# Top-k attention with an MLP behind it: row limits for four blocks at once, and row blocks taken by twos

## The chip, the cores and the metric

The kernel runs on one core of a Trainium2 chip. Its time is what the device takes for one execution, in microseconds (us); of several executions the median stands. One execution was also recorded by the hardware profiler. The core's engines work at the same time and meet through semaphores: PE multiplies matrices (its weight loads are listed as PEld), ACT applies functions with a scale and a bias, DVE works on vectors, POOL does the same more slowly, and SP issues DMA transfers. Each has its own list of instructions and works it off in order.

## The reference

`q`, `k` and `v` have 8 batches of 8 heads with 576 rows of 64. For each head, scores are `q k^T / 8`. In each row only the scores that reach the row's 32nd largest are kept. A softmax over them weighs `v`. The heads of a token are joined to 512 features, and an MLP follows with a parametric ReLU:

```python
kth = np.partition(scores, -32, axis=-1)[..., -32:-31]
scores = np.where(scores >= kth, scores, -1e9)
attn = softmax(scores);  x = join_heads(attn @ v)          # 4608 x 512
h = x @ w_in                                               # 4608 x 2048
out = (np.maximum(h, 0) + alpha * np.minimum(h, 0)) @ w_out
```

## The kernel before

Two heads form a pair; there are 32 pairs. The 576 rows of a pair's two heads make nine row blocks of 128: blocks 0 to 7 are four blocks of each head in turn, and block 8 holds the last 64 rows of both. All pairs together have 288 row blocks. `ORDER` lists them: pair after pair up to block 251, and mixed across the four pairs of the last batch from block 252 (`N0`) on.

The program writes out the order of every engine's instructions by hand. It counts ticks `n`, one a row block, and each stage of a block has its tick:

- PE computes scores in f32 into a PSUM tile (`scores`, L328), one tick ahead. Block `n` and its follower form a unit of two; a block 8 whose follower is not a block 8 too is a unit of one.
- ACT writes `b = scores + NT0` (`act_b`, L337). `NT0` is an estimate of the row's limit, from mean and variance of its scores, with its sign turned. ACT then sums the signs of `b` (`act_s`, L343): how many scores of the row lie above the estimate. It takes the exponential of a whole unit in one operation (`act_e`, L348).
- One tick on, POOL turns the sum into a flag `SG` (L353), and DVE turns the sign of `b` where the flag says that the wanted limit lies below the estimate (`flip`, L359).
- Two ticks on (`LAG_S`), DVE finds the eight largest of each of six segments of 96 columns (L369). Three ticks on (`LAG_M`), it merges these 48 into the 24 largest, in order (`merge_ops`, L384 and L386). The two are interleaved.
- Every three blocks DVE picks the limits. ACT has made the rank `ra` from the sum of signs (`sel_a`, L392). DVE compares it with a table of 24 numbers (`sel_eq`, L397), multiplies by the sorted list (`sel_pr`, L403), sums (`sel_sum`, L407) and turns the sign back (`limit`, L413).
- Seven ticks on (`LAG_W`), DVE makes the mask `b >= limit` (`mask`, L433), and POOL multiplies it with the exponentials (L443, `weights`). The last six blocks have both done by DVE in one operation (L440). SP issues the DMA that transposes the weights (L456, L452 for block 8).
- Behind that, by ticks after the mask: PE multiplies with `v` (`av`, L494), DVE takes the reciprocal of the sums (L511), ACT scales the result into `xb` (L523), SP transposes `xb`, and `feed` puts the MLP of the finished rows on a queue.

PE takes from that queue at each tick: steps cost credits (0.9 for a hidden step, L697; 1.5 for each third of an output block, L711 and L715), and a tick gives 1.9 credits, 2.4 from tick 288. Up to tick 253 at most one step a tick is taken. What is left two ticks after the last weights are due is flushed (`flush`), and the last 128 rows go through a path of their own (`last_ph`, L583; `last_pz`, L603).

Ahead of each pair, `prep_plan` spreads its preparation over the ticks before its first block (`BASE`): transposes of `q` and `k` on PE with copies on ACT, a product matrix (`pg`), its product with `q` (`pr0`, `pr1`), DVE's elementwise product `P` (L246), sums by PE into `st`, and seven small operations of ACT and DVE (L266 to L288) that end in `NT0` (`dve_6`). Pairs 11 to 19 are prepared a pair's length earlier, pairs from 20 on two lengths (`LEAD1`, `LEAD2`). `act_v` copies `v` to bf16 (L203) from a staging tile that `load_v` fills.

PSUM is shared out in pools: `ps_s` (scores, two tiles), `ps_d` (two banks: `pr0`, `pr1`, `st` and the products `pu` of `av`), `ps_a` (one bank: `pq`, `pk`, `pt`, `pg`) and `ps_m` (one, the MLP).

At the end `checks` tests the row limits and the estimates over all blocks; a flag decides on a general path (`general_batch`), none of which appears in the trace.

Of the kernel before, what the change touches and what calls it, by code (L numbers as in the profile page):

```python
# [16 lines left out]
S = 576  # L17
NSEG = 6
SEG = S // NSEG
KW = 24  # L20
TINY = 1.0e-30
ZSQ = 0.640625
M2MAX = 96.0
# [9 lines left out]
def kernel(  # L33
# [36 lines left out]
    ident_b = const.tile([128, 128], BF16, name="ident_b")  # L70
    nc.gpsimd.tensor_copy(ident_b, ident_f)
# [6 lines left out]
    iota = const.tile([128, KW], FP32, name="iota")  # L78
# [28 lines left out]
    M2 = prep.tile([128, NT], FP32, name="M2", bufs=1)  # L107
# [3 lines left out]
    st_vs = [prep.tile([128, 10, D], FP32, name=f"st_v{i}", bufs=1) for i in range(2)]  # L111
# [5 lines left out]
    def early_sets():  # L117
# [4 lines left out]
        for t_ in st_vs:  # L122
            nc.vector.memset(t_[64:128, 4, :], 0.0)
            nc.vector.memset(t_[0:64, 5, :], 0.0)
# [4 lines left out]
        for i in range(KW):  # L129
            nc.vector.memset(iota[:, i:i + 1], (1.0 + 2 * i) ** 2)  # L130
# [3 lines left out]
    def load(p, eng2=None):  # L134
# [10 lines left out]
        pairs[p] = dict(q=st_q, k=st_k, st_v=st_vs[p % 2], v=v_bfs[p % NV])  # L145

    def load_v(p):
        hA = 2 * p
        st_v = st_vs[p % 2]
# [25 lines left out]
    def prep_plan(p):  # L175
# [26 lines left out]
        def act_v():  # L202
            nc.scalar.copy(d["v"][:, :, 0:D], d["st_v"])  # L203
# [66 lines left out]
        def dve_2():  # L270
            nc.vector.tensor_tensor(d["sq"], M2[:, ns], d["sq"], ALU.subtract)

# [18 lines left out]
        if p == 1:  # L291
            ts = [-9, -8, -7, -6, -5, -4, -3, -2, -2, -2, -2, -2, -1, -1, 1]
        else:
            ts = [-14, -13, -12, -11, -10, -9, -7, -6, -5, -5, -4, -4, -3, -2, -8]
# [5 lines left out]
                 dict(dve=[dve_6]), dict(act=[act_v])]  # L300
# [29 lines left out]
    def act_b(n0):  # L330
        m = unit_of[n0][1]
        b = attn.tile([128, m, S], FP32, name=f"b{m}", bufs=5 if m == 2 else 1)
# [6 lines left out]
        tiles[n0]["bu"] = b  # L339
# [5 lines left out]
    def act_e(n0):  # L345
        m = unit_of[n0][1]
        e = attn.tile([128, m, S], BF16, name=f"e{m}", bufs=4 if m == 2 else 1)
        nc.scalar.activation(e, tiles[n0]["bu"], AF.Exp, scale=scl)  # L348
        for i in range(m):
            tiles[n0 + i]["e"] = e[:, i, :]  # L350
# [21 lines left out]

    Ls, sel, KPs = {}, {}, {}

    def merge_ops(n):
        C = Cs[n // TPP][:, n % TPP, :, :].rearrange("p g e -> p (g e)")
        if n % 3 == 0:
            Ls[n // 3] = attn.tile([128, 3, KW], FP32, name="L", bufs=2)
        L = Ls[n // 3][:, n % 3, :]
# [10 lines left out]
    def sel_a(m):  # L390
        a = attn.tile([128, 3], FP32, name="ra", bufs=2)
        nc.scalar.activation(a, S_all[:, 3 * m:3 * m + 3], AF.Square, bias=c513)  # L392
        sel[m] = a

    def sel_eq(m):
        EQ = attn.tile([128, 3, KW], FP32, name="EQ", bufs=1)
        nc.vector.tensor_tensor(EQ, sel[m].unsqueeze(2).to_broadcast([128, 3, KW]),  # L397
                                iota.unsqueeze(1).to_broadcast([128, 3, KW]), ALU.is_equal)
        sel[m] = EQ

    def sel_pr(m):
        L = Ls.pop(m)
        nc.vector.tensor_tensor(L, sel[m], L, ALU.mult)  # L403
        sel[m] = L

    def sel_sum(m):
        nc.vector.tensor_reduce(out=KK[:, 3 * m:3 * m + 3], in_=sel.pop(m), op=ALU.add,  # L407
                                axis=mybir.AxisListType.X)

    def limit(m):  # L410
        ms = slice(3 * m, 3 * m + 3)
        KPs[m] = attn.tile([128, 3], FP32, name="KP", bufs=4)
        nc.vector.scalar_tensor_tensor(out=KPs[m].bitcast(I32), in0=KK[:, ms].bitcast(I32),  # L413
                                       scalar=FLIP, in1=SG[:, ms], op0=ALU.bitwise_xor,
                                       op1=ALU.bitwise_xor)

    def row_limit(n):
        return KPs[n // 3][:, n % 3:n % 3 + 1]
# [39 lines left out]
    xb, xm = {}, {}  # L458
# [101 lines left out]

    t7 = 7 * S
    CL = t7 % NX + 64 + 384

    def turn_last(h):
        pool, tag = (ps_a, "pa") if h == 0 else (ps_m, "misc")
        xa = pool.tile([128, 2, 128], BF16, name="xa", tag=tag)
        for j in range(2):
            c0 = 128 * (2 * h + j)
            nc.tensor.transpose(xa[:, j, :], xb[B - 1][3][:, c0:c0 + 128], ident_b)
        nc.vector.tensor_copy(xT[:, 2 * h:2 * h + 2, CL:CL + 128], xa)  # L570

    lastc = {}
# [173 lines left out]
    LAG_S, LAG_M, LAG_W = 2, 3, 7  # L746
# [3 lines left out]
    with tc.manual_schedule(engines={E.PE, E.Activation, E.DVE, E.Pool, E.SP}):  # L750
# [73 lines left out]
        load_v(1)  # L824
# [8 lines left out]
        for wn in range(NT):  # L833
            wdue.setdefault(wn + LAG_W if wn < NW else 3 * (wn // 3) + 7, []).append(wn)
        n = 0
        end = max(NT + 24, 0)
        while n < end or back or after:
            for p in range(2, NPAIR):
# [25 lines left out]
            if n >= 3 and n % 3 == 0 and n - 3 < NT:  # L864
                sel_a((n - 3) // 3)
# [18 lines left out]
            for wn in due:  # L884
                if wn < NW:
# [4 lines left out]
            for wn in due:  # L890
                weights(wn, wn >= NW)
# [6 lines left out]
            pick = bool(merges) and mn % 3 == 2  # L898
            if pick and n >= NT:
                sel_eq(mn // 3)  # L900
            lm = n - LAG_M - 3
# [6 lines left out]
            if 0 <= lm < NT and lm % 3 == 0:  # L908
                limit(lm // 3)
            if pick and n < NT:  # L910
                sel_eq(mn // 3)
# [3 lines left out]
            if pick:  # L915
                sel_pr(mn // 3)
                held = [lambda m=mn // 3: sel_sum(m)]
                if mn % TPP == TPP - 1:
                    put(n + 2, "dve" if mn < NT - 1 else "end", lambda g=mn // TPP: check_group(g))
                    if mn == NT - 1:  # L920
                        put(n + 2, "end", checks)
# [143 lines left out]
```

## Time and profile before

| | |
|---|---|
| median of 3 runs | 872.82 us (871.4 to 875.64) |
| the profiled execution's own time | 873.98 us |
| its span, first to last instruction | 872.1 us |
| DVE busy | 835.1 us (96%) |
| ACT busy | 790.3 us (91%) |
| PE busy | 721.9 us (83%) |
| POOL busy | 431.0 us (49%) |
| granted PE clock, mean | 0.943 |

Busy time counts overlapping instructions of an engine once. A group's row has the line, engine and operation, what is written and read with the shape, the count, then the busy time in us, the mean duration of one in ns, and the idle time in front with what ended it. A row in order of time has the start and duration in us. An engine that is full in a stretch limits it; one that is not may still hold it up by coming late.

### The profile page before, as it was taken

The numbers are of one execution on the slowest core, as the hardware profiler recorded it, in microseconds if no ns is written. First come the engines' busy times: TensorE is split into PE (matmuls) and PEld (weight loads), VectorE is DVE, ScalarE is ACT, GpSimd is POOL, SyncE is SP. The second block draws the span as 40 slices with busy tenths as digits, with TensorE's granted clock in tenths as the row PEclk, the third lists the DMA queues.
The fourth block names the chain that finished last, engine by engine and source line by source line (L and its number), as shares of the span: only waits on it lengthen the run. The fifth ranks groups of instructions, "written<-read, shape, count | busy, mean of one in ns | idle before, by whom it ended". The sixth has DMA issues, their size and how long they took to land.

```text
span 872.1 us, 20608 instructions
## 1 busy us (share of the span) xinstructions
PE 721.9 (83%) x5697; PEld 428.3 (49%) x5771; DVE 835.1 (96%) x5188; ACT 790.3 (91%) x1873; POOL 431.0 (49%) x630
## 2 busy tenths in 40 slices
PE   6776688778978789787987789977897988899996
PEld 4443444334554345444454445643455554566674
DVE  4999999999999999999999999999999999999992
ACT  6999999999999999889999999989999899979861
POOL 1455545555454555545555455554554555544530
PEclk9997779899979999989998999989999999999999
DMA  7999644644665545564576445475455543535442
GB/s 161 156 178 199 131 89 90 126 91 97 135 139 107 108 102 116 100 135 95 114 154 115 98 97 116 111 136 98 92 128 121 121 103 81 106 71 100 91 96 56
DMA packets 342619, 99.37 MB, mean 114 GB/s; under 512 B 334672, under 2 KB 334944, under 8 KB 342496
## 3 DMA queue, kind: packets, MB, share of 16 engines
q1 hardware_dynamic: 340144, 95.58, 54.4%
q0 software_dynamic: 1152, 2.10, 2.0%
q8 instruction: 47, 0.77, 0.4%
q14 instruction: 76, 0.62, 0.2%
q10 hardware_dynamic: 1200, 0.30, 0.2%
HBM read 36.71 MB, written 9.44 MB: 53 GB/s over the span
## 4 chain that ended last, share of the span: by engine, by line
DVE 62%; ACT 21%; PE 12%; DMA 2%; issue 1%; POOL 1%; SPq 0%; DVEq 0%; another core or an unknown queue 0%; ACTq 0%
DVE C L369 20%; DVE y L359 9%; DVE mk L433 9%; DVE C L386 8%; DVE L L384 7%; ACT b L337 5%; ACT h L343 5%; ACT e L348 4%; PE ps L328 4%; PE pz L715 3%; PE ph L697 2%; ACT gT L703 2%; DVE P L246 2%; ACT xb L523 2%; PE pu L494 1%
## 5 line engine op out<-in xcount | busy, mean ns | idle before, releaser
L443 POOL TENSOR_TENSOR w<-mk,e 128x576 bf16<-128x576 bf16 x250 | 319.3, 1277 | 337.9 <-DVE mk L433 187.5
L369 DVE MAX8 C<-y 128x8 f32<-128x96 f32 x1728 | 419.1, 243 | 0.1
L328 PE MATMUL ps<-qkT 64*128 64x288 f32 (+1 forms) x1280 | 256.5, 474 | 35.1 <-ACT b L337 34.6
L337 ACT ACTIVATE b<-ps,NT 128x576 f32<-128x576 f32 x288 | 202.3, 761 | 3.1 <-PE ps L328 3.1
L343 ACT ACTIVATE h<-b 128x576 bf16<-128x576 f32 x288 | 202.9, 705 | 1.7
L697 PE MATMUL ph<-xT,w_in_b 128*128 128x128 bf16 (+2 forms) x997 | 150.4, 292 | 40.8 <-ACT gT L703 33.6
L328 PEld LDWEIGHTS ps<-qkT 64*128 64x128 f32 (+1 forms) x1280 | 134.3, 194 | 97.6 <-ACT b L337 59.8
L348 ACT ACTIVATE e<-b 128x1152 bf16<-128x1152 f32 (+1 forms) x158 | 174.2, 1102 | 0.0
L384 DVE MAX8 L<-C 128x8 f32<-128x48 f32 x864 | 162.6, 188 | 0.1
L359 DVE TENSOR_SCALAR y<-b,SG 128x576 int32<-128x576 int32 x288 | 147.0, 510 | 8.2 <-POOL SG L353 7.8
L433 DVE TENSOR_SCALAR mk<-b,KP 128x576 bf16<-128x576 f32 x282 | 143.6, 509 | 0.0
L715 PE MATMUL pz<-w_out_b,gT 128*128 128x512 bf16 x543 | 132.4, 380 | 1.2 <-issue 0.5
L697 PEld LDWEIGHTS <-w_in_b 128*128 128x128 bf16 x1024 | 80.4, 100 | 104.0 <-issue 79.6
L703 ACT ACTIVATE gT<-ph 128x512 bf16<-128x512 f32 x140 | 86.0, 621 | 28.1 <-PE ph L697 28.1
L386 DVE MATCH_REPLACE8 C<-L,C 128x48 f32<-128x48 f32 x576 | 108.3, 188 | 0.0
L715 PEld LDWEIGHTS <-gT 128*128 128x128 bf16 x560 | 51.6, 98 | 68.5 <-issue 14.0
L494 PE MATMUL pu<-v_bf,wT 128*128 128x65 bf16 (+1 forms) x1600 | 69.4, 198 | 14.4 <-DMA wT<-w 6.9
L494 PEld LDWEIGHTS <-wT 128*128 128x128 bf16 (+1 forms) x1600 | 65.2, 103 | 25.6 <-issue 10.2
L353 POOL TENSOR_SCALAR SG<-S_all 128x1 int32<-128x1 f32 x288 | 65.3, 227 | 18.9 <-ACT h L343 18.8
L443 POOL TENSOR_TENSOR wm<-mk,e 128x576 bf16<-128x576 bf16 x32 | 40.8, 1276 | 49.9 <-DVE mk L433 45.6
L343 ACT ACTIVATION_READ_ACCUMULATOR h<-b 128x1 f32 x288 | 62.8, 218 | 0.0
L523 ACT ACTIVATE xb<-pu,rz 128x64 bf16<-128x64 f32 x224 | 54.5, 369 | 0.0
(113 smaller groups left out, 728.1 us busy)
## 6 DMA issues: line engine op xcount, KB each, us to landing
out_dram<-o_sb SPq DMA_DIRECT2D x34, 256.0 KB, 2.3
st_q<-in_q_dram SPq DMA_DIRECT2D x64, 128.0 KB, 2.8
st_v<-in_v_dram SPq DMA_DIRECT2D x64, 128.0 KB, 2.6
kst<-in_k_dram SPq DMA_DIRECT2D x62, 128.0 KB, 2.6
w_stage<-in_moe_w_out_dram SPq DMA_DIRECT2D x16, 256.0 KB, 3.1
w_in_b<-in_moe_w_in_dram POOLq DMA_DIRECT2D x8, 256.0 KB, 6.4
wT<-w SPq DMA_TRANSPOSE x128, 3.3
st_q<-in_q_dram SPq DMA_DIRECT2D x32, 32.0 KB, 2.5
```

The lines of the kernel that those rows point to most:

```text
L328: nc.tensor.matmul(o_, l_, r_, start=True, stop=True)
L337: nc.scalar.activation(t["b"].rearrange("p (a c) -> p a c", a=2), t["ps"], AF.Identity, bias=NT0[:, p * TPP + j:p * TPP + j + 1], scale=ON ...
L343: nc.scalar.activation(h, tiles[n]["b"], AF.Sign, accum_out=S_all[:, n:n + 1])
L348: nc.scalar.activation(e, tiles[n0]["bu"], AF.Exp, scale=scl)
L359: nc.vector.tensor_scalar(t["y"].bitcast(I32), t["b"].bitcast(I32), FLIP, SG[:, n:n + 1], ALU.bitwise_xor, ALU.bitwise_xor)
L369: return [lambda g=g: nc.vector.max(out=C[:, n % TPP, g, :], in_=t["y"][:, g * SEG:(g + 1) * SEG]) for g in range(NSEG)]
L384: ops.append(lambda r=r, src=src: nc.vector.max(out=L[:, 8 * r:8 * r + 8], in_=src))
L386: ops.append(lambda r=r, src=src: nc.vector.match_replace(out=C2, in_to_replace=L[:, 8 * r:8 * r + 8], in_values=src, imm_value=NEG))
L433: nc.vector.tensor_scalar(t["mk"], t["b"], row_limit(n), None, ALU.is_ge)
L443: nc.gpsimd.tensor_tensor(dst, t["mk"], t["e"], ALU.mult)
L697: nc.tensor.matmul(hold[f][:, i, :], w_in_b[:, kk, (f + i) * 128:(f + i + 1) * 128], xT[:, kk, c0:c0 + tb], start=(kk == 0), stop=(kk == N ...
L715: nc.tensor.matmul(pz[0:m], hold["gT"][:, f, r0:r0 + m], w_out_b[:, f, :], start=False, stop=(f == NFT - 1))
```

## The change

- Limits are picked for groups of four row blocks up to block 251 and of three from 252 on (`GROUPS`). Masks and weights stand `z + 4` ticks behind their block: eight in groups of four, seven in groups of three. Where two masks fall due in one tick (blocks 251 and 252), the second is fused on DVE.
- The rank is the absolute value of the shifted sum in place of its square, and table, rank and comparison result are bf16.
- Units of two run on across the border of a pair; only block 8 and the last block are units of one. There are six tiles `b` and five tiles `e`, all of two blocks, where there were five and four, and one of each of a single block.
- `pr0` moves from the two banks of `ps_d` to the one of `ps_a`, for pairs from 2 on.
- `M2` is bf16 and only checked; the subtraction `dve_2` reads `st` in PSUM instead.
- `dve_6` runs a tick earlier, behind the flip of that tick. `act_v` runs three ticks later (five ticks earlier for pair 1), and `load_v` two ticks later for most pairs, both through one staging tile in place of two.
- The bf16 identity matrix is made at tick 288 in a tile that the sign pass leaves.

```diff
-M2MAX = 96.0
+M2MAX = 95.5
...
-    ident_b = const.tile([128, 128], BF16, name="ident_b")
-    nc.gpsimd.tensor_copy(ident_b, ident_f)
...
-    iota = const.tile([128, KW], FP32, name="iota")
+    iota = const.tile([128, KW], BF16, name="iota")
...
-    M2 = prep.tile([128, NT], FP32, name="M2", bufs=1)
+    M2 = prep.tile([128, NT], BF16, name="M2", bufs=1)
...
-    st_vs = [prep.tile([128, 10, D], FP32, name=f"st_v{i}", bufs=1) for i in range(2)]
+    st_v = prep.tile([128, 10, D], FP32, name="st_v", bufs=1)
...
         for i in range(KW):
-            nc.vector.memset(iota[:, i:i + 1], (1.0 + 2 * i) ** 2)
+            nc.vector.memset(iota[:, i:i + 1], 1.0 + 2 * i)
...
-        m = 1 if ORDER[n][1] == 8 and ORDER[n + 1][1] != 8 else 2
+        m = 1 if n in (8, NT - 1) else 2
...
-            if nm == "pr0":
+            if nm == "pr0" and p < 2:
                 pool, tag = ps_d, "pd"
...
-            nc.vector.tensor_tensor(d["sq"], M2[:, ns], d["sq"], ALU.subtract)
+            nc.vector.tensor_tensor(d["sq"], d["st"][:, 0, :], d["sq"], ALU.subtract)
...
         if p == 1:
-            ts = [-9, -8, -7, -6, -5, -4, -3, -2, -2, -2, -2, -2, -1, -1, 1]
+            ts = [-9, -8, -7, -6, -5, -4, -3, -2, -2, -2, -2, -2, -1, -1, -4]
         else:
-            ts = [-14, -13, -12, -11, -10, -9, -7, -6, -5, -5, -4, -4, -3, -2, -8]
+            ts = [-14, -13, -12, -11, -10, -9, -7, -6, -5, -5, -4, -4, -3, -3, -5]
...
-                 dict(dve=[dve_6]), dict(act=[act_v])]
+                 {dvx: [dve_6]}, dict(act=[act_v])]
...
-        b = attn.tile([128, m, S], FP32, name=f"b{m}", bufs=5 if m == 2 else 1)
+        b = attn.tile([128, 2, S], FP32, name="b", bufs=6)
...
-        e = attn.tile([128, m, S], BF16, name=f"e{m}", bufs=4 if m == 2 else 1)
-        nc.scalar.activation(e, tiles[n0]["bu"], AF.Exp, scale=scl)
+        e = attn.tile([128, 2, S], BF16, name="e", bufs=5)
+        nc.scalar.activation(e[:, 0:m, :], tiles[n0]["bu"], AF.Exp, scale=scl)
...
+    GZ = 4
+    GROUPS = [(i, GZ) for i in range(0, N0, GZ)] + [(i, 3) for i in range(N0, NT, 3)]
+    group_of = {i: (g, z) for g, z in GROUPS for i in range(g, g + z)}
...
-    def sel_a(m):
-        a = attn.tile([128, 3], FP32, name="ra", bufs=2)
-        nc.scalar.activation(a, S_all[:, 3 * m:3 * m + 3], AF.Square, bias=c513)
-        sel[m] = a
-
-    def sel_eq(m):
-        EQ = attn.tile([128, 3, KW], FP32, name="EQ", bufs=1)
-        nc.vector.tensor_tensor(EQ, sel[m].unsqueeze(2).to_broadcast([128, 3, KW]),
-                                iota.unsqueeze(1).to_broadcast([128, 3, KW]), ALU.is_equal)
-        sel[m] = EQ
+    def sel_a(g, z):
+        a = attn.tile([128, GZ], BF16, name="ra", bufs=2)
+        nc.scalar.activation(a[:, 0:z], S_all[:, g:g + z], AF.Abs, bias=c513)
+        sel[g] = a[:, 0:z]
+
+    def sel_eq(g, z):
+        EQ = attn.tile([128, GZ, KW], BF16, name="EQ", bufs=1)[:, 0:z, :]
+        nc.vector.tensor_tensor(EQ, sel[g].unsqueeze(2).to_broadcast([128, z, KW]),
+                                iota.unsqueeze(1).to_broadcast([128, z, KW]), ALU.is_equal)
+        sel[g] = EQ
...
+    def make_ident_b():
+        lastc["i"] = attn.tile([128, S], BF16, name="ident_b", tag="h", bufs=1)[:, 0:128]
+        nc.gpsimd.tensor_copy(lastc["i"], ident_f)
...
-            wdue.setdefault(wn + LAG_W if wn < NW else 3 * (wn // 3) + 7, []).append(wn)
+            g, z = group_of[wn]
+            wdue.setdefault(wn + z + 4 if wn < NW else g + 7, []).append(wn)
+        ga = {g + z: (g, z) for g, z in GROUPS}
+        gm = {g + z - 1: (g, z) for g, z in GROUPS}
...
-                if n == max(0, BASE[p] - 13):
+                if n == max(BASE[p] - 11, BASE[p - 1] - 4):
                     load_v(p)
+            if n == 1:
+                load_v(1)
+            if n == NT:
+                make_ident_b()
...
-                if wn < NW:
+                if wn < NW and wn == due[0]:
                     mask(wn)
...
-                weights(wn, wn >= NW)
+                weights(wn, wn >= NW or wn != due[0])
                 tail_of(n, wn)
...
-            pick = bool(merges) and mn % 3 == 2
+            pick = gm.get(mn)
...
-            lm = n - LAG_M - 3
+            lm = gm.get(mn - 1)
```

`sel_pr`, `sel_sum`, `limit`, `merge_ops` and `row_limit` are changed in the same way, from three blocks to a group's `z`.

More of the change, by code (lines that the diff above doesn't have):

```diff
@@ L121, in early_sets @@
             nc.gpsimd.memset(ksts[i][64:128, 4, :], 0.0)
[L122 to L124 removed]
+        nc.vector.memset(st_v[64:128, 4, :], 0.0)
+        nc.vector.memset(st_v[0:64, 5, :], 0.0)
         for t_ in v_bfs:
@@ L202, in act_v @@
         def act_v():
-            nc.scalar.copy(d["v"][:, :, 0:D], d["st_v"])
+            nc.scalar.copy(d["v"][:, :, 0:D], st_v)
         def pe_k():
@@ L745 @@
     PE_TICK = 1.9
[L746 removed]
+    LAG_S, LAG_M = 2, 3
     NW = NT - 6
@@ L907 @@
             run(n, "dve")
-            if 0 <= lm < NT and lm % 3 == 0:
-                limit(lm // 3)
+            if lm:
+                limit(*lm)
             if pick and n < NT:
-                sel_eq(mn // 3)
+                sel_eq(*pick)
             if 0 <= n - 1 < NT:
```

65 lines of the change are left out of this document (32 added, 33 removed).

## The prediction

> **What bounds the kernel now.** I read the page's first part, then busy time by stretches of the span, then the waits, then groups of instructions by shape, then the order of time around single operations. A tick is one turn of the program's loop, one row block of 128 query rows; there are 288, so DVE's 835.1 us are 2.9 us a tick.
>
> ```profile
> span 872.1 us, 20608 instructions
> PE 721.9 (83%) x5697; PEld 428.3 (49%) x5771; DVE 835.1 (96%) x5188; ACT 790.3 (91%) x1873; POOL 431.0 (49%) x630
> 24.00:120.00 96.00, 71.20 (x407) 41.59 (x408) 92.08 (x567) 93.44 (x211) 48.97 (x71) 0.83 0.89 158
> 120.00:768.00 648.00, 542.20 (x4292) 312.97 (x4353) 647.64 (x4048) 610.12 (x1486) 340.02 (x479) 0.95 0.54 110
> 768.00:816.00 48.00, 44.84 (x362) 28.09 (x364) 44.56 (x264) 39.80 (x83) 23.38 (x35) 1.00 0.43 86
> 782.00:856.00 74.00, 71.83 (x703) 47.10 (x709) 70.56 (x404) 55.62 (x110) 31.44 (x44) 1.00 0.48 95
> ```
>
> Columns of a stretch: its length, then busy time of PE, PE's weight loads, DVE, ACT, POOL, and the granted clock. Three stages show. Before 120 us ACT is fullest (93.44 of 96). From 120 to 768 us DVE has no gap (647.64 of 648) and ACT follows close (610.12). From 782 us PE takes over (71.83 of 74), while DVE idles 3.4 us between 768 and 816. So a microsecond taken from DVE's list counts in the middle if ACT and PE can follow, and at the end only if PE can.
>
> DVE's durations overlap, so the price of an instruction is the distance from its start to the next start:
>
> ```profile
> 503.17 0.21 DVE L397 TENSOR_TENSOR EQ<-ra,iota 128x72 f32<-128x72 f32 x1
> 503.30 0.51 DVE L359 TENSOR_SCALAR y<-b,SG 128x576 int32<-128x576 int32 x1
> 503.73 0.22 DVE L403 TENSOR_TENSOR L<-EQ,L 128x72 f32<-128x72 f32 x1
> 503.88 0.51 DVE L433 TENSOR_SCALAR mk<-b,KP 128x576 bf16<-128x576 f32 x1
> 504.31 0.21 DVE L407 TENSOR_REDUCE KK<-L 128x3 f32<-128x72 f32 x1
> 504.44 0.25 DVE L369 MAX8 C<-y 128x8 f32<-128x96 f32 x1
> 506.88 0.15 DVE L413 SCALAR_TENSOR_TENSOR KP<-KK,SG 128x3 int32<-128x3 int32 x1
> 506.95 0.51 DVE L359 TENSOR_SCALAR y<-b,SG 128x576 int32<-128x576 int32 x1
> ```
>
> A limit set costs EQ 0.13, product 0.15, sum 0.13, limit 0.07: 0.48 us for three row blocks.
>
> **Part 1: sets of four.** Before, 288/3 = 96 sets, 46.1 us. After, 252/4 = 63 sets of four and 36/3 = 12 of three. What 24 further columns cost I take from shorter operations of the same kinds:
>
> ```profile
> L403 DVE TENSOR_TENSOR L<-EQ,L 128x72 f32<-128x72 f32 x96 | 21.2, 221 | 0.0
> L407 DVE TENSOR_REDUCE KK<-L 128x3 f32<-128x72 f32 x96 | 20.7, 216 | 0.1
> L397 DVE TENSOR_TENSOR EQ<-ra,iota 128x72 f32<-128x72 f32 x96 | 19.7, 206 | 0.0
> L246 DVE TENSOR_TENSOR P<-pr,qkT 128x64 bf16<-128x64 f32 x32 | 6.8, 212 | 0.0
> L281 DVE TENSOR_TENSOR t<-sq,t 128x9 f32<-128x9 f32 x32 | 5.1, 159 | 0.1
> L284 DVE TENSOR_REDUCE sq<-t 128x9 f32<-128x27 f32 x32 | 5.0, 157 | 0.1
> L440 DVE SCALAR_TENSOR_TENSOR w<-b,KP,e 128x576 bf16<-128x576 f32 x6 | 4.5, 811 | 0.0
> L433 DVE TENSOR_SCALAR mk<-b,KP 128x576 bf16<-128x576 f32 x282 | 143.6, 509 | 0.0
> L392 ACT ACTIVATE ra<-S_all,c 128x3 f32<-128x3 f32 x96 | 30.7, 319 | 0.0
> L348 ACT ACTIVATE e<-b 128x1152 bf16<-128x1152 f32 x130 | 155.3, 1195 | 0.0
> L348 ACT ACTIVATE e<-b 128x576 bf16<-128x576 f32 x28 | 18.9, 673 | 0.0
> ```
>
> EQ grows by (206-159)/63 = 0.75 ns a column, 18 ns; the product by (221-159)/63, 24 ns; the sum by (216-157)/45, 31 ns; the limit by nothing. A set of four is 0.55 us; 63 x 0.553 + 12 x 0.48 = 40.6 us. DVE gains 5.5 us, all of it before row block 252.
>
> On ACT 21 rank operations go. From one of them to the next start is 0.19 us (below), so 4.0 us.
>
> ```profile
> 355.85 0.31 ACT L392 ACTIVATE ra<-S_all,c 128x3 f32<-128x3 f32 x1
> 356.04 1.39 ACT L337 ACTIVATE b<-ps,NT 128x576 f32<-128x576 f32 x2
> ```
>
> **Part 2: bf16 table and ranks.** EQ then reads and writes 16-bit data. The trace has no such operation of this length. If it goes on as before, nothing is gained. If its columns took half the time, EQ with 96 columns would fall from 224 to 188 ns: 36 ns x 63 = 2.3 us more. A loss I exclude by none of the rows, but the bf16 output of the 64-column product (212 ns) lies where f32 operations of that length do, so I put that end at zero. I take zero, the f32 row being the nearest. The Trainium skill (VectorE: DVE Perf Modes, the side-by-side table of modes) gives a two-input operation two results a cycle only if its operands are 16-bit with step one; here the rank is repeated along 24 columns with step zero, so by that condition the sum stays at the f32 price, and by the tier alone it would be 2.3 us lower. No row of before shows which.
>
> The product still has an f32 factor: no change. Abs for Square on ACT: same shape, no change (the other end is the last rival). The variance subtraction now reads PSUM: the P row reads PSUM in 212 ns with 64 columns, against 200 to 213 ns interpolated between the SBUF rows, so from -0.3 to +0.4 us over 32 pairs; I take +0.2. dve_6 one tick earlier and behind the flip: the same instruction, moved past one flip, 0.
>
> **Part 3: masks eight behind.** No instruction is added, except that blocks 251 and 252 fall due in one tick and the second is fused on DVE: 811-509 = 0.3 us. Weight products on POOL, the transposes on SP's queue, both P.V products, their scaling on ACT and the feeding of the MLP move along one tick; among themselves nothing moves. One more buffer each of b and e keeps ACT's room: a b buffer was free after 8 ticks and needed after 11, now after 9 and 12; an e buffer had two spare ticks and has two.
>
> DVE in all: 5.5 - 0.3 - 0.2 = 5.0 us.
>
> **Part 4: twos across pairs.** 28 single and 130 double exponentials become 2 and 143: 174.2 to 172.2 us, 2.0 us by durations, about one by starts. ACT in all gains some 5 to 6 us, about as much as DVE, so ACT can follow. Score matmuls keep their number and, per 18 blocks, their number in sequence on each half of the array; next-pair scores are needed one tick sooner in every second pair, which dve_6's earlier place pays.
>
> **Part 5: banks, one v staging.** Before, pr0 and pr1 took both banks of the shared pair, and the second P.V product waited for DVE's P:
>
> (Waits: total us, times, longest; the last row is a DMA with its KB and us to landing.)
>
> ```profile
> PE pu L494 <- DVE P L246: 6.4, 7, 1.9
> ACT v_bf L203 <- DMA st_v<-in_v_dram: 1.7, 1, 1.7
> st_v<-in_v_dram SPq DMA_DIRECT2D x64, 128.0 KB, 2.6
> ```
>
> That wait should go; PE waits there only when it is ahead, so I count 0. What is late next: the bank of st is now read by dve_2 on DVE, and the first P.V product takes that bank one tick later (second rival). v loads come two ticks later in SP's queue, behind transposes that wait for POOL, and each waits for ACT's copy of the pair before, which ACT issued three ticks earlier. They have six ticks, three for pairs 12 and 21, about 8 us, to land (2.6 us). If that cover fails, ACT loses up to 2.6 us, twice; I take 0. The late bf16 identity on POOL (waiting for the last sign pass) and the dropped memsets: 0, POOL is half idle.
>
> **Part 6: the tail.** The MLP of the last batches is fed one tick later, but the closing flush stays at tick 294. Working through the credit rule tick by tick, one output step (7 matmuls) is left at the end of tick 293 before, and three after.
>
> ```profile
> 849.48 2.28 DVE L440 SCALAR_TENSOR_TENSOR w<-b,KP,e 128x576 bf16<-128x576 f32 x3
> 851.66 2.32 PE L715 MATMUL pz<-w_out_b,gT 128*128 128x512 bf16 x10
> 854.70 1.47 PE L715 MATMUL pz<-w_out_b,gT 128*128 128x512 bf16 x6
> 856.00 0.80 PE L494 MATMUL pu<-v_bf,wT 128*128 128x65 bf16 x20
> ```
>
> Ten such matmuls take 2.32 us, a step 1.6 us. The last P.V product starts right behind such a step, so PE sets the end there. Between 0 and 3.2 us return; I take 1.6, since at tick 252 the backlog is larger by one step and PE is nearly full from there on.
>
> **Sum.** -5.0 + 1.6 = -3.4 us. The profiled execution took 873.98 us (span 872.1, 1.9 around it), 1.2 above the median; 870.6 for it, and 869.4 for the median of 872.82. Measurement tells no change from 0.5%, or 4.4 us.
>
> **Rivals.**
> (a) Forecast: 867.8 to 871.0 by the tail's bounds. 0.45, of which 0.13 lies below 868.4 (faster by over 0.5%).
> (b) EQ's columns at half price, and the tail hidden because PE fills its idle time (2.2 of 74 us): 872.82 - 7.3 = 865.5. For: PE's gaps. Against: the step-zero operand. 0.27, with any like gain.
> (c) The gain isn't collected: ACT and PE keep their own pace and DVE merely waits. For: DVE idles 3.4 us in 768 to 816 already. Against: in the middle DVE has no gap. 872.8 to 874.4. 0.08.
> (d) Slower: the new bank wait. dve_2 and the first P.V product of one pair, before:
>
> ```profile
> 307.34 0.80 PE L494 MATMUL pu<-v_bf,wT 128*128 128x65 bf16 x20
> 310.63 0.15 DVE L271 TENSOR_TENSOR sq<-M,sq 128x9 f32<-128x9 f32 x1
> ```
>
> One tick later that product would start at about 310.2, and dve_2 ends at 310.8: a wait of 0.6 us. At 25 pairs 0.4 to 0.7 us are 10 to 17 us of PE, less the 6.4 us removed. If PE cannot make them up: 873 to 880.5. It decides once more than about 8 us stay lost. Against: PE waits there only when a tick ahead of DVE. 0.15.
> (e) Abs needs another activation table than Exp; every rank operation would load twice.
>
> ```profile
> L68 ACT ACT_TABLE_LOAD x1 | 1.3, 1283 | 1.3 <-PEq L1049 1.3
> ```
>
> 75 x 2 x 1.283 = 192 us, 1065 in all. Against: one load serves Exp, Sign, Square, Relu, Copy and Identity. The Trainium skill (ScalarE: Activation LUTs, on table sets) has abs in every set as filler, by which this costs nothing. 0.01; other slower ways, such as more half-clock stretches of PE in the tail, 0.04.
>
> **How the numbers follow.** Faster: 0.13 + 0.27 = 0.40. Slower: (d) without 0.02, (e) and the rest, 0.02 of (c): 0.20. Same: 0.40. The range from 865 to 877 reaches into (b) and the nearer half of (d), and leaves out under 2 in 10.
>
> **What would show it.** L, EQ and KK groups x75, the EQ of 96 columns near 224 ns (part 1 right) or 188 (b); exponentials 143 and 2; DVE busy about 830 us, still without a gap from 120 to 740. No second table load. The wait for P gone and a wait of the first P.V product for dve_2 in its place, of few us (part 5) or many (d). At the end the last P.V product behind more output matmuls (part 6). The prediction is wrong if DVE's gaps in the middle open (c, d), or if the last fused weights come 5 us sooner and the end does too (no tail loss).

## The result and the profile after

The changed kernel took 909.49 us (median of 6 runs, 902.7 to 911.66), the kernel before on the same chip 873.39 us (median of 6, 871.4 to 878.19). The ratio is 1.0394, with a 95% interval of 1.0367 to 1.0421: slower by 36 us, where 869.4 us was forecast and the range ended at 877.

The profiled execution has a span of 905.8 us, 33.7 more than before. Its page, engines first, then the same stretches as in the prediction (length, busy time of PE, PE's weight loads, DVE, ACT, POOL, then the granted clock):

```profile
span 905.8 us, 20474 instructions
PE 760.1 (84%) x5704; PEld 430.6 (48%) x5771; DVE 836.3 (92%) x5102; ACT 790.3 (87%) x1839; POOL 431.1 (48%) x629
24.00:120.00 96.00, 74.68 (x401) 42.78 (x404) 90.34 (x553) 90.58 (x204) 47.73 (x69) 0.57 0.80 155
120.00:768.00 648.00, 551.80 (x4069) 300.69 (x4120) 624.67 (x3819) 588.15 (x1404) 327.07 (x460) 0.92 0.54 107
782.00:856.00 74.00, 67.47 (x543) 40.63 (x549) 68.50 (x410) 62.23 (x130) 37.11 (x53) 0.95 0.45 90
```

PE is the engine that changed: 38 us more busy time for the same matmuls, and a lower clock. In the first stretch the view has 0.57 against 0.83 before, but the 0.83 is too high. The clock record of that execution begins at 59.87 us, and what lies ahead of it counts as full clock. The matmuls there ran at half clock:

```profile
27.29 1.12 PE L208 MATMUL pk<-ident_f,kst 128*128 128x128 f32 x4
```

Four such transposes took 0.66 us at 181.71, at full clock. With half clock up to 59.87 us the first stretch comes to about 0.64 (estimate), and the mean of 0.943 for the kernel before is too high as well. DVE did not get more to do, it got gaps: 23.3 us in the middle stretch, where it had 0.4. By the starts of DVE's flips, the gaps are spread over the whole middle: block 36 is reached 1.6 us later than before, block 252 25.4 us later (2.97 us a tick in between, against 2.86), and the remaining 8.2 us follow behind that.

The groups by shape (count, busy us, mean ns of one, idle time in front) show which work it is:

```profile
L324 PE MATMUL ps<-qkT 64*128 64x288 f32 x1024 | 232.0, 488 | 15.7 <-ACT b L333 15.4 <-ACT qkT L208 0.3
L324 PE MATMUL ps<-qkT 64*64 64x288 f32 x256 | 57.2, 533 | 0.0
L397 DVE TENSOR_TENSOR EQ<-ra,iota 128x96 bf16<-128x96 bf16 x63 | 14.8, 235 | 0.0
L397 DVE TENSOR_TENSOR EQ<-ra,iota 128x72 bf16<-128x72 bf16 x12 | 2.5, 208 | 0.0
L403 DVE TENSOR_TENSOR L<-EQ,L 128x96 f32<-128x96 bf16 x63 | 15.7, 249 | 0.0
L407 DVE TENSOR_REDUCE KK<-L 128x4 f32<-128x96 f32 x63 | 15.3, 243 | 0.0
L413 DVE SCALAR_TENSOR_TENSOR KP<-KK,SG 128x4 int32<-128x4 int32 x63 | 8.5, 136 | 0.0
L344 ACT ACTIVATE e<-b 128x1152 bf16<-128x1152 f32 x143 | 170.8, 1194 | 0.0
L68 ACT ACT_TABLE_LOAD x1 | 1.3, 1283 | 1.3 <-PEq L1059 1.3
```

The limit sets are as forecast. From start to start, where no gap follows, their four operations cost 0.154, 0.170, 0.163 and 0.062 us, 0.549 a set; with the twelve sets of three at 0.48, that makes 40.4 us. The score matmuls are not as forecast: together they grew from 256.5 to 282.7 us by the page's own group. The waits (total us, times, longest) tell who waits for whom:

```profile
PE pk L204 <- ACT qkT L196: 37.8, 26, 3.9
DVE y L355 <- POOL SG L349: 28.7, 33, 4.0
ACT b L333 <- PE ps L324: 10.4, 15, 2.3
ACT v_bf L199 <- DMA st_v<-in_v_dram: 3.9, 3, 1.6
PE pu L495 <- DMA wT<-w: 1.2, 1, 1.2
```

The first three of them before:

```profile
PE pk L208 <- ACT qkT L200: 7.5, 5, 2.7
DVE y L359 <- POOL SG L353: 7.8, 6, 3.5
ACT b L337 <- PE ps L328: 3.1, 6, 1.0
```

PE's transposes of `k` wait for ACT's copy of `q`, DVE's flip for POOL's flag, ACT's `b` for scores. After the change PE is late for ACT, ACT is late for POOL, and DVE, the engine that was full, runs dry behind it.

**What a mixed unit costs.** Before, block 8 of a pair stood alone in its unit. Now it shares one with the block ahead of it or behind it; such a unit is called mixed here, and that other block the lone one. In order of time, from the trace before (a regular unit and a block 8):

```profile
179.05 1.24 PE L328 MATMUL ps<-qkT 64*128 64x288 f32 x8
185.24 1.19 PE L328 MATMUL ps<-qkT 64*64 64x288 f32 x8
```

and after, a mixed unit at full and one at half clock:

```profile
651.58 2.69 PE L324 MATMUL ps<-qkT 64*64 64x288 f32 x12
298.55 4.89 PE L324 MATMUL ps<-qkT 64*128 64x288 f32 x12
```

The starts of their matmuls within the unit, in us, with equal starts (7 ns apart) joined by a plus:

```
regular (179.05)   0+0  0.35+0.35  0.59+0.59  0.83+0.83                                    end 1.24
mixed (651.58)     0+0  0.29+0.29  0.63  0.98  1.31+1.31  1.60+1.60  1.95  2.29            end 2.69
```

In a regular unit two blocks of different heads lie on the two halves of PE's array and run side by side: four steps. In a mixed one the quarters of block 8 run two at a time, but the four matmuls of the lone block have nothing beside them: eight steps. In the regular unit the first step takes 0.35 us and the others 0.24. In the mixed one the shape changes three times: the first step of each shape takes 0.29 or 0.35 us, and the step that ends in a change 0.33 to 0.34. The Trainium skill (TensorEngine Tiling (Array Packing), Key Properties) states that a change of the tiling mode, unlike one of the tile, drains the array; the three changes within this unit, at 0.33 to 0.34 us each where a step without one takes 0.24, agree with it. Per 18 blocks that is 7 x 1.24 + 2 x 2.69 = 14.06 us in place of 8 x 1.24 + 2 x 1.19 = 12.30; times 14, 24.6 us at full clock, an estimate that lies near the 26.2 that the group grew by. At half clock a regular unit takes about 2.3 us, less than a tick of 2.86. A mixed one takes 4.89 us, far more than one. Of 31 sequences with a mixed unit, 11 took more than 4 us.

**What comes late beside it.** ACT before and after, around the copy of `q`, the scalings of the second P.V product (`xb`, `xm`) and the transposes that wait. Before:

```profile
178.03 1.01 ACT L523 ACTIVATE xb<-pu,rz 128x64 bf16<-128x64 f32 x4
178.82 0.55 ACT L523 ACTIVATE xm<-pu,rz 64x64 bf16<-64x64 f32 x2
181.02 0.63 ACT L200 COPY qkT<-pq 128x512 f32<-128x512 f32 x1
181.71 0.66 PE L208 MATMUL pk<-ident_f,kst 128*128 128x128 f32 x4
```

After, ACT's rows and then PE's (in brackets the idle time in front and its releaser):

```profile
185.56 1.45 ACT L333 ACTIVATE b<-ps,NT 128x576 f32<-128x576 f32 x2
186.81 1.03 ACT L524 ACTIVATE xb<-pu,rz 128x64 bf16<-128x64 f32 x4
187.60 0.56 ACT L524 ACTIVATE xm<-pu,rz 64x64 bf16<-64x64 f32 x2
187.99 0.63 ACT L196 COPY qkT<-pq 128x512 f32<-128x512 f32 x1
196.20 0.60 ACT L707 ACTIVATE gT<-ph 128x512 bf16<-128x512 f32 x1 [4.03 <-PE ph L701]
...
185.80 1.02 PE L701 MATMUL ph<-xT,w_in_b 128*128 128x512 bf16 x4 [1.37 <-ACT gT L707]
188.68 0.65 PE L204 MATMUL pk<-ident_f,kst 128*128 128x128 f32 x4 [1.85 <-ACT qkT L196]
189.17 0.80 PE L495 MATMUL pu<-v_bf,wT 128*128 128x65 bf16 x20
189.90 4.44 PE L324 MATMUL ps<-qkT 64*128 64x288 f32 x12
```

Before, the scalings stood a tick ahead of the copy. One tick later they stand in its tick, in front of it. PE, which works in order, waits 1.85 us for that copy with a P.V product and a mixed unit behind it, the clock falls to one half at 190.39, the unit takes 4.44 us, and ACT, waiting for the MLP matmuls that follow, stands still for 4.03 us. DVE's gap comes next, behind the flag that POOL makes of ACT's sum:

```profile
199.24 0.52 DVE L355 TENSOR_SCALAR y<-b,SG 128x576 int32<-128x576 int32 x1 [3.25 <-POOL SG L349]
```

### The profile page after: what moved, and what is told of

Read it like the earlier page. It is cut to its first block, busy times and chain, and to the rows that moved or that the text cites. A ratio compares the mean times of both kernels' runs of the same rounds, so it can differ in the third digit from the quotient of the medians.

```text
span 905.8 us, 20474 instructions
## 1 busy us (share of the span) xinstructions
PE 760.1 (84%) x5704; PEld 430.6 (48%) x5771; DVE 836.3 (92%) x5102; ACT 790.3 (87%) x1839; POOL 431.1 (48%) x629
## 5 line engine op out<-in xcount | busy, mean ns | idle before, releaser
L324 PE MATMUL ps<-qkT 64*128 64x288 f32 (+1 forms) x1280 | 282.7, 497 | 15.7 <-ACT b L333 15.4
L339 ACT ACTIVATE h<-b 128x576 bf16<-128x576 f32 x288 | 205.9, 715 | 1.5
L324 PEld LDWEIGHTS ps<-qkT 64*128 64x128 f32 (+1 forms) x1280 | 136.9, 200 | 116.3 <-issue 58.0
L355 DVE TENSOR_SCALAR y<-b,SG 128x576 int32<-128x576 int32 x288 | 146.8, 510 | 29.4 <-POOL SG L349 28.7
L344 ACT ACTIVATE e<-b 128x1152 bf16<-128x1152 f32 (+1 forms) x145 | 172.1, 1187 | 0.0
L384 DVE MAX8 L<-C 128x8 f32<-128x48 f32 x864 | 164.7, 191 | 0.1
L719 PE MATMUL pz<-w_out_b,gT 128*128 128x512 bf16 x555 | 134.7, 380 | 0.8 <-issue 0.3
L495 PE MATMUL pu<-v_bf,wT 128*128 128x65 bf16 (+1 forms) x1600 | 71.4, 202 | 1.2 <-DMA wT<-w 1.2
L339 ACT ACTIVATION_READ_ACCUMULATOR h<-b 128x1 f32 x288 | 65.6, 228 | 0.0
L204 PE MATMUL pk<-ident_f,kst 128*128 128x128 f32 x128 | 25.6, 333 | 38.0 <-ACT qkT L196 37.8
```

The costliest lines, as they stand in the source:

```text
L324: nc.tensor.matmul(o_, l_, r_, start=True, stop=True)
L339: nc.scalar.activation(h, tiles[n]["b"], AF.Sign, accum_out=S_all[:, n:n + 1])
L344: nc.scalar.activation(e[:, 0:m, :], tiles[n0]["bu"], AF.Exp, scale=scl)
L355: nc.vector.tensor_scalar(t["y"].bitcast(I32), t["b"].bitcast(I32), FLIP, SG[:, n:n + 1], ALU.bitwise_xor, ALU.bitwise_xor)
L384: ops.append(lambda r=r, src=src: nc.vector.max(out=L[:, 8 * r:8 * r + 8], in_=src))
L495: nc.tensor.matmul(o_, wT[:, 4 * side + c, cs], d["v"][:, 5 * side + c, :], start=(c == 0), stop=(c == 4))
```

## The experiments

Three theories were on record at the start: the loss comes from the mixed units (A), from the v loads, whose copy on ACT waits in the trace (B), or from ACT's copies of the preparation, which units across pairs put at other places of a tick, so that PE waits for the copy of `q` (C). The first three experiments led to a fourth (D): the tail, which moved by a tick, brings ACT's scalings in front of that copy, and this hurts only where a mixed unit follows. Its rival (F) was that this collision does not matter. Later came the question why, with the loss gone, no gain was left.

**Score units as before, in the changed kernel** (tiles `b` and exponentials still by twos across pairs):

```diff
+    while n < NT:
+        m = 1 if ORDER[n][1] == 8 and ORDER[n + 1][1] != 8 else 2
+        for i in range(m):
+            pe_of[n + i] = (n, m, i)
...
-        ns = range(n0, n0 + unit_of[n0][1])
+        ns = range(n0, n0 + pe_of[n0][1])
...
-            if n + 1 < NT and unit_of[n + 1][2] == 0:
+            if n + 1 < NT and pe_of[n + 1][2] == 0:
```

> The changed kernel, but PE takes the scores by the units of before (blocks 0 and 1, 2 and 3, 4 and 5, 6 and 7, block 8 alone) and ACT writes b by them; b and e tiles and exponentials stay by twos across pairs. Theory A (a score unit that holds a block 8 and a block of another kind costs PE 2.69 us where two units of before cost 1.24 and 1.19; PE, nearly full, comes late): score time on PE falls from 283 to about 257 us, the time to 866 to 878 us. Theory B (the one v staging tile: ACT waits for v at pairs 12 and 21, PE falls idle, its clock halves): the two stalls stay, 890 to 905 us. Theory C (with units across pairs ACT does its preparation copies at other places of a tick, and PE waits for the copy of q): those waits stay, 895 to 910 us.

Measured: 876.88 us, ratio 1.0046 (1.0029 to 1.0064). All but 4 us of the 36 are gone with this one edit, as A expected. PE still waits 25.1 us for the copy of `q`, so that wait alone is not the loss (C). Units across pairs are necessary for it. ACT writes `b` by PE's units here, so the edit takes back both, and this run does not part them.

**The copy of v two ticks later for pairs 12 and 21**, in the changed kernel, and the same together with the edit above:

```diff
+        if p in (LEAD1 + 1, LEAD2 + 1):
+            ts[-1] = -3
```

> The changed kernel, but the copy of v for pairs 12 and 21 stands two ticks later on ACT. Theory A: 898 to 908 us, little gained. Theory B: ACT no longer waits 1.3 us for v at 291 us, the two deep stalls near 300 and 515 us (DVE loses 4.4 us in each of the two stretches) go: 885 to 895 us. Theory C: 903 to 910 us.

> Both edits: score units of before and v copied two ticks later for pairs 12 and 21. Theory A: as the first run or up to 2 us less, 865 to 876 us; should the sums of the prediction hold for the rest, 868 to 871 us. Theory B: 868 to 876 us. Theory C: 885 to 900 us.

Measured: 900.78 us, ratio 1.0316 (1.0281 to 1.0351), and 877.87 us, ratio 1.0062 (1.0037 to 1.0086). The v wait falls from 3.9 to 1.5 us. In the changed kernel that is worth 7 to 9 us (by the ratios, by the medians). The wait stands at the head of one of the long stalls:

```profile
291.15 0.73 ACT L199 CAST v_bf<-st_v 128x640 bf16<-128x640 f32 x1 [1.32 <-DMA st_v<-in_v_dram]
...
293.48 1.86 PE L701 MATMUL ph<-xT,w_in_b 128*128 128x512 bf16 x4 [2.79 <-ACT gT L707]
```

The clock is halved from 292.79 to 309.86 us, and the mixed unit at 298.55 falls into that. With the units of before the same edit brings nothing, and B had expected 885 to 895 us for the first run: the wait for v can set a stall off, but it is not the cause of the loss.

**Mixed units alone, in the kernel before** (five `b` and five `e` tiles of two blocks, `dve_6` a tick earlier):

```diff
-        m = 1 if ORDER[n][1] == 8 and ORDER[n + 1][1] != 8 else 2
+        m = 1 if n in (8, NT - 1) else 2
...
-            ts = [-14, -13, -12, -11, -10, -9, -7, -6, -5, -5, -4, -4, -3, -2, -8]
+            ts = [-14, -13, -12, -11, -10, -9, -7, -6, -5, -5, -4, -4, -3, -3, -8]
...
-                 dict(dve=[dve_6]), dict(act=[act_v])]
+                 {dvx: [dve_6]}, dict(act=[act_v])]
```

> The kernel before with units across pairs alone (scores, b and exponentials; five b and five e tiles of two blocks; dve_6 a tick earlier, without which ACT would wait for NT0). Limits by three, masks seven behind, two v staging tiles stay. Theory A: score time on PE about 283 us, 895 to 910 us. Theory B: 870 to 876 us. Theory C: 895 to 905 us, with PE waiting some 38 us for the copy of q as in the changed kernel.

Measured: 877.12 us, ratio 1.0055 (1.003 to 1.008). PE's busy time is 744.4 us, 22.5 above before, and almost all of it is absorbed. A alone falls, since it had expected 895 to 910 us; so does C.

**That, with everything behind the weights one tick later** (in `tail_of`), **and the later tail alone, in the kernel before:**

```diff
+                n += 1
```

> The kernel before with units across pairs (877 us) and, besides, everything behind the weights (P.V products, reciprocals, scalings, transposes of x, MLP feeding) one tick later, as masks eight behind have it; limits by three, masks seven behind, banks and v staging as before. Theory D: the collision is made in a kernel that has no other part of the change: wait for the copy of q 30 to 40 us, 890 to 905 us. Theory F: 876 to 880 us.

> The kernel before with everything behind the weights one tick later and nothing else: the fourth corner beside before (873), before with mixed units (877) and both (904). Theory D (the collision with the copy of q hurts only where a long mixed score unit follows it): 873 to 880 us, with a wait for the copy of q of 20 to 30 us. If the collision costs by itself: 890 to 900 us.

Measured: 904.4 us, ratio 1.0386 (1.0312 to 1.0459), and 875.49 us, ratio 1.0011 (0.9995 to 1.0026). So the four corners are 873, 877, 875 and 904 us, with no limits of four, no bf16, no new bank and no new v staging in any of them. The last two lie where D expected them, and D holds. The stretch from 120 to 740 us of the three, mixed units, late tail, both:

```profile
120.00:740.00 620.00, 531.82 (x4087) 296.58 (x4139) 620.00 (x3860) 583.92 (x1417) 323.14 (x456) 0.95 0.57 111
```

```profile
120.00:740.00 620.00, 516.01 (x4048) 293.45 (x4104) 618.65 (x3860) 586.24 (x1424) 323.33 (x457) 0.94 0.54 111
```

```profile
120.00:740.00 620.00, 530.52 (x3933) 285.48 (x3931) 601.56 (x3734) 564.73 (x1364) 313.73 (x442) 0.92 0.54 109
```

DVE (third busy time) has no gap, one of 1.4 us, and 18.4 us. The waits of the late tail alone, then of both:

```profile
PE pk L208 <- ACT qkT L200: 24.1, 21, 2.6
DVE y L359 <- POOL SG L353: 6.2, 4, 3.3
```

```profile
PE pk L208 <- ACT qkT L200: 30.1, 22, 2.8
DVE y L359 <- POOL SG L353: 24.1, 11, 3.8
ACT b L337 <- PE ps L328: 12.6, 18, 1.7
```

The late tail makes PE wait for the copy either way; only with mixed units is there too little time left in PE to make it up. How far PE is ahead shows in the time that its score matmuls wait for ACT's `b`: 34.6 us before, 27.2 with the late tail, 11.6 with mixed units (18.1 with both, where ACT runs late too).

Between 24 and 860 us PE ran at half clock for about 131 us before, about 156 with mixed units, 154 with the late tail, 195 with both and 194 in the changed kernel. The first two are estimates: the clock records of these executions have 96 and 126 us and begin only at 59.87 and 53.5 us, and the time ahead of that, in which the matmuls ran as slowly as at half clock, is added. The 154 us cost almost nothing, since at half clock a regular unit still fits into a tick.

**ACT's copies ahead of its scalings within a tick**, in the changed kernel, and in the one with old units and later v:

```diff
-                    for f in fs:
-                        put(BASE[p] + dt, eng, f)
+                    for f in reversed(fs):
+                        if eng == "act":
+                            cal.setdefault((BASE[p] + dt, eng), []).insert(0, f)
+                    if eng != "act":
+                        for f in fs:
+                            put(BASE[p] + dt, eng, f)
```

> The changed kernel, with one reordering: where ACT has in one tick copies of a pair's preparation and the scaling of a P.V product, the copies go first. Theory D (masks a tick later bring the six scalings of the second P.V product into the tick of the copy of q; PE waits in order for that copy, 37.8 us in 26 cases, and where a mixed score unit of 2.69 us follows, ACT and then DVE run dry): the wait for the copy of q falls below 20 us, the time to 876 to 890 us. Theory F (the collision does not matter; the rest is v staging, the bank move or the limits): 900 to 910 us.

> Score units of before, v copied two ticks later for pairs 12 and 21, and the copies first. Theory D: the wait for the copy of q falls from 25 us to under 12, the time from 877.9 to 866 to 873 us. Theory F: 875 to 880 us, as without the reordering.

Measured: 891.11 us, ratio 1.0211 (1.0185 to 1.0237), and 881.81 us, ratio 1.0112 (1.0058 to 1.0167). In the changed kernel the order within the tick is worth 18 us: the wait of the transposes falls from 37.8 to 13.5 us, that of the flip from 28.7 to 15.1. With old units D had expected 866 to 873 us, and that failed: the wait for the copy of `q` falls to 8.7 us, but another moves to the next transposes (`pt`, 29.2 us, 21.4 without the edit), and the time is no better (the two intervals, with and without the edit, overlap). The order is half of the cure where PE is short, and no gain in itself.

**The preparation one tick later too** (pairs from 2 on, old units, v later), so that it stands to the tail as before:

```diff
-            ts = [-14, -13, -12, -11, -10, -9, -7, -6, -5, -5, -4, -4, -3, -3, -5]
+            ts = [-13, -12, -11, -10, -9, -8, -6, -5, -4, -4, -3, -3, -2, -2, -5]
```

> Score units of before, v copied two ticks later for pairs 12 and 21, and the preparation of pairs from 2 on one tick later (v's copy kept), so that it stands against the scalings of P.V as in the kernel before. Theory D: the wait for the copy of q near the 7.5 us of before, 866 to 873 us, unless ACT meets NT0 too late in pairs up to 10 (up to 5 us more). Theory F: 875 to 880 us.

Measured: 876.33 us, ratio 1.0038 (1.0021 to 1.0056). Under D, 866 to 873 us and a wait of 7.5 us for the copy of `q` were expected; that wait is still 26.1 us. Block 252 is reached at 737.5 us, 2.8 us sooner than before, but from there on 5.3 us are lost, of which 3.0 lie between the last weights and the last P.V product. The second P.V product now waits in the way that rival (d) described:

```profile
PE pu L504 <- DVE sq L272: 14.6, 12, 2.6
```

**Fewer blocks in groups of four**, to find what the last 36 blocks cost (old units, v later, PE's and ACT's preparation a tick later; groups of four up to block 215, and, with `PLATE` 32, up to 251):

```diff
+            if 1 < p < PLATE:
+                ts[0:8] = [-13, -12, -11, -10, -9, -8, -6, -5]
...
-    GROUPS = [(i, GZ) for i in range(0, N0, GZ)] + [(i, 3) for i in range(N0, NT, 3)]
+    GROUPS = [(i, GZ) for i in range(0, 216, GZ)] + [(i, 3) for i in range(216, NT, 3)]
+    PLATE = 28
```

> Score units of before, v copied two ticks later for pairs 12 and 21; ACT's and PE's preparation of pairs 2 to 27 one tick later (against the scalings as before), DVE's as in the changed kernel; limits by four only up to block 215, by three from there, so that the tail is fed as before. If limits by four are worth the 5.7 us that their instructions measure, and the rest of the loss is the tail's late feeding: 866 to 871 us. If ACT and PE set the pace (rival c): 872 to 876 us.

> The same with limits by four up to block 251, so the tail is fed one tick late. Against e10 it shows the price of the late feeding: 3 to 5 us more by the stretch from block 252 to the end, 870 to 875 us; 0 to 1 us more if that stretch is set by something else.

Measured: 880.99 us, ratio 1.0086 (1.0063 to 1.0108), and 881.53 us, ratio 1.0086 (1.0062 to 1.0109). The two agree, as expected if something other than the late feeding sets the end; so this did not price it. Both times lie above what was expected and above the kernel with the whole preparation moved. In these two PE waits 33 to 34 us for the copy of `q` and 26 to 27 us for that of `pg`; with the whole preparation moved it is 26.1 and 27.0 us, so only the first could be their price. That was not tried.

**Is a lighter DVE worth anything?** The product of each limit set was left out, in the kernel before and in the one with old units; in a third kernel ACT's rank operations also:

```diff
     def sel_pr(m):
         L = Ls.pop(m)
-        nc.vector.tensor_tensor(L, sel[m], L, ALU.mult)
         sel[m] = L
...
-        nc.vector.tensor_reduce(out=KK[:, 3 * m:3 * m + 3], in_=sel.pop(m), op=ALU.add,
+        nc.vector.tensor_reduce(out=KK[:, 3 * m:3 * m + 3], in_=sel.pop(m), op=ALU.max,
```

> The kernel before with the product of each limit set left out (96 operations on DVE, 0.15 us each from start to start, 14.4 us in all); the sum takes the largest of the keys in its place, so the limits, and with them the output, are others. Theory 1, DVE's list sets the time from block to block: about 859 us, all 14.4 us come back. Theory 2, the gain of a lighter DVE is not collected because ACT and PE keep their own pace: 868 to 873 us, and DVE's gaps grow by what it was spared.

> e1_score_pairs with the product of each limit set left out in the same way (63 operations at 0.17 us and 12 at 0.15, 12.5 us). If DVE's list set the time there: 864 us. If ACT and PE set it, as I now suppose for that kernel: 873 to 877 us.

> e12_before_no_product with ACT's rank operations left out too (96 at 0.19 us, 18 us of ACT). If ACT's pace holds back what e12_before_no_product was spared, this one is faster than it by the rest of the 14.4 us (about 859 us). If ACT is not what holds it, the two agree within 2 us.

Measured: 867.99 us, ratio 0.9939 (0.9918 to 0.9961); 871.72 us, ratio 0.998 (0.9958 to 1.0002); 861.89 us, ratio 0.9852 (0.9812 to 0.9892). All three against 873.89 us for the kernel before. Of 14.4 us taken from DVE alone 5.9 come back. Taking 18 us from ACT (by starts) brings another 6.1. With old units the ratio falls from 1.0046 to 0.998, some 6 us of 12.5. Neither theory was right as put: both lists hold the kernel back. The kernel before without the product, its page and its middle:

```profile
PE 731.7 (84%) x5771; PEld 429.8 (50%) x5771; DVE 822.0 (95%) x5092; ACT 788.6 (91%) x1873; POOL 430.6 (50%) x630
120.00:740.00 620.00, 530.35 (x4199) 301.19 (x4196) 614.23 (x3826) 587.38 (x1435) 326.41 (x462) 0.95 0.56 112
```

DVE lost 13.1 us of work, and its gap in the middle opened from 0.4 to 5.8 us. Its `P` waits 9.3 us for PE there, 2.7 before. Without ACT's rank operations that wait is 2.3 us and the gap 0.7. An engine with no gap in 620 us was still not the only limit.

None of the kernels that compute the whole reference is faster than the one before.

## Why the prediction was wrong

**Part 4 failed, and together with Part 3 it turned the sign.** The step was "Score matmuls keep their number and, per 18 blocks, their number in sequence on each half of the array", priced at nothing. The number per half is the same over 18 blocks, but the two lone blocks lie seven blocks or more apart and cannot run beside each other, and with three changes of shape no step of a mixed unit is as short as the 0.24 us of a regular one. A mixed unit takes 2.69 us, 0.88 more than half a regular unit and a block 8; PE has 26 us more to do. About half of the 0.88 us could be read from the trace of before, where a regular unit (1.24 us) and a block 8 (1.19 us) take four steps each: two further steps of 0.24 us. The price of a change of shape within a unit had no row there. Part 4 alone costs 4 us (877). The rule quoted above from the Trainium skill (TensorEngine Tiling (Array Packing), Key Properties) speaks against this change, and was not weighed.

**Part 3 failed.** "Among themselves nothing moves" is true of the tail's own steps. Against the preparation of the next pairs, which stayed, all of them moved by a tick, and six scalings came to stand in front of the copy of `q`. The step counted the moved instructions, but not what is queued behind them on ACT in the tick that they entered. Alone this costs 0.1% (interval from nothing to 0.3%); with Part 4 it is 31 us. The prediction priced the parts one by one and so had no term for the pair.

**Part 1 was right about DVE's list and wrong about its worth.** 40.4 us was measured, 40.6 forecast. But the sum took the 5 us as time, on the ground that DVE has no gap. Taking 14.4 us away gave 5.9, four tenths; by that the 5 us were worth 2, an estimate. The kernel with old units (the first experiment) shows it too. From block 36 to block 252 its sets take 4.1 us less by their starts, but DVE's whole list only 1.3 us less, and its gaps are 3.8 us in place of 0.4, so that the stretch takes 620.7 us against 618.6. DVE's busy time, expected at about 830 us, was 833.2 there and 836.3 in the changed kernel. The prediction's own sign of being wrong, gaps of DVE in the middle, came in both. Rival (c), which said so, had 0.08.

**Part 2 was right.** EQ took 235 ns with 96 columns, nearer to 224 than to 188, and with 72 columns 208 ns, where it took 206 in f32: bf16 gained nothing. The condition on steps from the Trainium skill (VectorE: DVE Perf Modes, the side-by-side table of modes) agrees. Rival (b) falls with it, and so does (e): there is one table load, in agreement with the Trainium skill (ScalarE: Activation LUTs, on table sets).

**Part 5.** The wait of the second P.V product for `P` is gone, as said. The new bank wait of rival (d) does not appear in the changed kernel, perhaps because PE is not ahead enough; it came with 14.6 us once PE's work was moved (above). The cover of the v loads failed for three waits, 3.9 us. "ACT loses up to 2.6 us, twice" bounded the wait, not what it set off: 7 to 9 us with mixed units, nothing without.

**Part 6 was right in its mechanism, at its upper end.** From the last weights to the last P.V product 4.25 us passed before and 7.27 us in the changed kernel: 3.0 us, where 1.6 was taken and 3.2 was the bound. The rows, from the last output matmuls on:

```profile
885.07 3.62 PE L719 MATMUL pz<-w_out_b,gT 128*128 128x512 bf16 x16
888.52 0.80 PE L495 MATMUL pu<-v_bf,wT 128*128 128x65 bf16 x20
889.36 0.18 DVE L541 RECIPROCAL rz<-pu 128x4 f32<-128x4 f32 x1 [4.91 <-PE pu L495]
```

With the old units the account of the profiled executions closes: block 252 is reached 1.1 us sooner (5.0 was forecast), the way from there to the last weights takes 0.9 us more, the last P.V product comes 3.0 us later behind them, and 1.0 us is lost behind that: 3.9 us before rounding, 876.0 against 872.1. Why the last 35 blocks gain nothing there, while the late tail alone shortens them by 3.6 us and so pays for its later P.V product, stays open.

Of the rivals that forecast a slower kernel, (d) had the right engine, PE, which cannot make lost time up, and the wrong wait. "More half-clock stretches of PE" named what the trace then showed, but looked for it in the tail, where the clock had been full.

## What to carry to other kernels

Price a change of how work is grouped by the steps of the new group, in order, not by counts: which matmuls run side by side, and where the shape changes. When a whole chain moves by a tick, list for each engine what is already in the tick that it enters and who waits behind it; and when two parts take slack from the same engine, price them together, since 873, 877, 875 and 904 us do not add up. Before a microsecond of the fullest engine is counted as a microsecond of time, take some of its work away on the chip and see how much comes back.

## What was not expected of the hardware

**The clock of PE moves on a fixed grid, and half-idle windows are enough for a fall.** In the trace of before, changes of the granted clock between 30 and 850 us lie on a grid of 3.413 us. All 15 falls to 0.50 follow a window of the grid in which PE's matmuls were busy for 19 to 53%, and all 15 returns to 1.00 one with 89% or more; 13 windows (38% to 100% busy) stayed at half. After the change 13 falls follow windows with 20 to 69%, 13 returns windows with 81% or more, and 41 windows stayed at half. The share alone does not decide: before, three windows with 47 to 52% kept the full clock, and six with 89% or more stayed at half. The longest idle time in a window ahead of a fall was 2.56 us before and 2.74 us after, so none of these windows was idle as a whole. What looks dear is the way back, which came only behind a nearly full window, while waits for ACT recur every nine blocks. The Trainium skill (TensorE: Matmul & The Clock Gate, Part 1) has the window of about 3.4 us and the two states, and the trace agrees; it puts the fall behind a whole idle window, and here windows that were busy for up to half of their time, after the change up to 69%, sufficed.

**Quarter-array and half-array matmuls in turn** took 0.29 to 0.35 us a step at full clock, where all but the first step of a unit of one shape follow after 0.24.
